# Another memory layout for the low magnitude rows and the short exponential tables of an S4 mixer kernel, and a written-down instruction sequence

## The chip, the cores and the metric

One NeuronCore of one Trainium2 chip runs the whole kernel. Its engines have instruction queues of their own and run side by side: TensorE (PE, whose weight loads are the row PEld), VectorE (DVE), ScalarE (ACT), GpSimd (POOL, nearly unused here) and SyncE (SP, which issues transfers). Each engine takes its queue strictly in order. The metric is the device time of one execution in microseconds.

## The reference

The input `x` has 2048 positions of 512 channels. It is normalised, and two branches work on the result.

- Branch A is a state-space convolution. Each channel `d` has 128 complex modes `n`, and its kernel is `K[d, l] = Re sum_n C[d,n] dB[d,n] exp(dt[d] A[d,n] l)` for `l = 0..2047`. The normalised input is convolved with `K` (in the reference with FFTs of length 4096), and `Dskip * u` is added.
- Branch B is a mixer with an MLP: layer norm, a 512x512 product, GELU, a shift of four channel groups by +1, -1, +2, -2 positions, a second 512x512 product and a residual; then layer norm, a product to 1376 features, GELU, a product back to 512 and a residual.

The output is `x + A * silu(B)`.

## The kernel before

**Stages.** The kernel first normalises, runs branch B's token mixing (`token_mixing`) and the first stage of the transform of the input (`u_stage1`, `u_spectra`). `tables(0)` and `tables(1)` build the kernel `K` for the two halves of the channels, each in eight chunks (`cc`) of 32 channels. `mlp(g)` is the MLP for one of eight groups of 256 positions; its products are two-part f16 products (`w3h`, `w4h`, `ghl`, `x1T`). `kstage1` and `products` transform `K` and multiply the spectra; `inverse` and `finish` come last.

**Tables.** The modes lie on the 128 partitions. A position is split in a coarse part, `256 a + 64 b` with a = 0..7 and b = 0..3, and a fine part of 64 values, so that the sum over modes becomes 64 small products per chunk (PE `pc<-pt`), of coarse factors with fine factors. Every factor is a magnitude (an exponential, from ACT) times a sine or cosine. The magnitudes are made once for a block of 128 channels, four blocks in all, by `block`:

- `mag` holds 64 rows of 128 channels, as two tiles of 32 rows: `mag[0]` (rows 0 to 31, the low rows) and `mag[1]` (rows 32 to 63). In each, row `4 b + c` of channel `q` stands at `[b, q, c]`: four rows lie side by side in memory, and the next channel is four words on. `exps` computes 40 of the 64 rows, each with one exponential of 128 channels, which writes every fourth word. `squares` makes the other 24 from these by squaring, in four instructions.
- `EB` holds 12 exponentials of 128 channels: `ea` (8 coarse steps a, with a innermost) and `eb` (4 steps b, with b innermost). `eb` is then multiplied by the mode's weight `wmr` (DVE `EB<-EB,par`).

Each chunk uses them on DVE: `factors` multiplies `ea` by `eb` (DVE `pt<-EB`, 1024 elements), and `sums` multiplies fine cosines and sines by `mag`. The four products of a chunk have 1024 elements each: `kf[:, low]` and `pf[:, low]` with `mag[0]`, `kf[:, mid]` with `mag[1]` (these three are DVE `TENSOR_TENSOR pt<-mag,pt`), and `pf[:, mid]` with `mag[1]` (DVE `SCALAR_TENSOR_TENSOR pt<-mag,pt`). Their outputs run over `[b, q, c]`, c innermost, because the matmuls read one channel at a time. The products' line in the profile is that of the helper that issues every instruction (L515), so tiles name the work.

**Order.** Nothing runs as the program records it. `Plan` records operations (some 1730) with their dependencies; `order` then gives each an engine and a place; `issue` writes each engine's queue in that order. Some operations can go to ACT or DVE (`Either`: copies, scalings by a constant, absolute values), some stores to SP or ACT. Before the change, `order` is a list scheduler: whenever an engine is free it takes, among the operations whose inputs are done by its own estimates, the one with the smallest due time in a table `DUE`, with extra costs for a change of ACT's table and preferences for DVE or ACT:

```
t, e = min(
    (max(free[e], min(o.ready for o in pool)), e) for e, pool in pools.items() if pool
)
...
if pick is None or (v, o.idx) < score:
    pick, score = o, (v, o.idx)
```

`order` also adds filler matmuls (`<-ident`, L514) where it expects PE to idle. Its cost for a DVE operation (`dve_cost`) knows nothing of memory layout; that of an ACT operation (`act_cost`) knows the step of the output.

Of the kernel before, what the change touches and what calls it, by code (L numbers as in the profile page):

```python
# [10 lines left out]
F32 = mybir.dt.float32  # L11
# [8 lines left out]
P = 128  # L20
# [16 lines left out]
BQ = 128  # L37
# [55 lines left out]
class Op:  # L93
    __slots__ = (
        "eng", "alts", "calls", "cost", "deps", "succ", "table", "vt", "idx", "nbytes", "n", "ready", "start",
        "alias", "first", "last", "psum", "mode", "stage", "dma", "room", "fresh", "free_at", "fill",
# [23 lines left out]
SHIFT, KEEP = 0.09, 1.0  # L120
# [6 lines left out]
DUE = (  # L127
# [129 lines left out]
)  # L257
SWITCH = 20.74
PREFERP, AVOIDP = 12.42, -13.86
PREFER, AVOID = -0.38, -5.84  # L260

# [1266 lines left out]
```

## Time and profile before

| | |
|---|---|
| median of 3 runs | 562.91 us (561.33 to 565.46) |
| the profiled execution's own time | 561.96 us |
| its span, first to last instruction | 560.2 us |
| PE busy / DVE busy / ACT busy | 533.4 / 466.1 / 410.2 us |
| granted TensorE clock, mean | 0.983 |
| ACT table loads | 49, 1283 ns each |

The profiled execution lies 0.95 us below the median of the runs; 1.76 us of its time lie outside the span. In the rows, a tile's buffer numbers are left out, `128x1024 f32` is partitions by elements, and "mean ns" is an instruction's own duration: on DVE and ACT the next instruction starts somewhat before the last one ends, so instructions in a row stand closer than their durations. Busy time in a stretch counts such overlap once.

### The profile page before, as it was taken

What the parts mean: (1) busy time and instruction counts of PE and PEld (TensorE: products, weight loads), DVE (VectorE), ACT (ScalarE), POOL (GpSimd) and SP (SyncE); (2) the same over time, 40 slices, a digit from 0 to 9 for tenths busy, and PEclk for the clock granted to TensorE, in tenths of its full rate; (3) what the DMA queues carried; (4) which work ended last, traced back from release to release, by engine and by line L of the source; (5) the groups of instructions that cost most, each with busy time, mean ns of one, the idle gap of its engine ahead of it and who ended that gap; (6) DMA issues with size and microseconds to landing.
All of it is one profiled execution on the core that took longest, in us unless ns stands there. A gap on an engine that the chain in (4) does not pass through costs nothing.

```text
span 560.2 us, 14282 instructions
## 1 busy us (share of the span) xinstructions
PE 533.4 (95%) x6104; PEld 349.6 (62%) x6104; DVE 466.1 (83%) x710; ACT 410.2 (73%) x588; POOL 0.7 (0%) x6
## 2 busy tenths in 40 slices
PE   7989999989899899999999999999999999999982
PEld 7967677855344466656766666676676665675630
DVE  5999999999999998999999999999415168564276
ACT  2999997999987998998899999768246235224420
POOL 0000000000000000000000000000000000000000
PEclk9999999999999899999999999999999999999995
DMA  9975667535647252735333431453886669859947
GB/s 205 229 214 190 233 222 253 180 117 165 196 143 263 96 140 68 217 140 186 112 100 100 133 131 60 142 162 124 264 281 236 225 190 281 254 156 277 327 130 223
DMA packets 69695, 103.14 MB, mean 184 GB/s; under 512 B 14784, under 2 KB 48832, under 8 KB 68736
## 3 DMA queue, kind: packets, MB, share of 16 engines
q1 hardware_dynamic: 68864, 100.13, 57.8%
q10 hardware_dynamic: 768, 2.10, 1.2%
q8 instruction: 48, 0.79, 0.6%
q14 instruction: 15, 0.12, 0.1%
HBM read 64.46 MB, written 37.75 MB: 182 GB/s over the span
## 4 chain that ended last, share of the span: by engine, by line
PE 72%; DVE 15%; ACT 5%; DMA 5%; issue 2%; SPq 1%; DVEq 0%; ACTq 0%
PE pb L515 29%; PE pa L515 21%; PE pd L515 11%; PE pc L515 11%; DVE pt L515 9%; DVE X L515 3%; DMA X<-in_A_u_dram 2%; ACT mag L515 2%; DMA w<-in_B_w_dram 2%; ACT pt L515 1%; DVE w4h L515 1%; SPq L515 1%; ACT L512 1%; DVE w3h L515 1%; DMA out_dram<-X 0%
## 5 line engine op out<-in xcount | busy, mean ns | idle before, releaser
L515 PE MATMUL pb<-x1T,w3h 128*128 128x256 f16 (+1 forms) x1056 | 123.4, 273 | 2.7 <-issue 1.2
L515 PE MATMUL pa<-w4h,ghl 128*128 128x512 f16 (+1 forms) x528 | 121.7, 379 | 0.0
L515 PEld LDWEIGHTS <-w3h 128*128 128x128 f16 (+1 forms) x1056 | 102.6, 100 | 28.5 <-issue 13.9
L515 PEld LDWEIGHTS <-ghl 128*128 128x128 f16 (+1 forms) x528 | 49.9, 98 | 59.7 <-issue 7.5
L515 DVE SCALAR_TENSOR_TENSOR ghl<-g,wsc,ghl 128x512 f16<-128x512 f32 (+1 forms) x48 | 33.6, 700 | 41.7 <-ACT ghl L515 41.6
L512 ACT ACT_TABLE_LOAD x49 | 62.9, 1283 | 7.4 <-DMA out_dram<-X 5.8
L515 PE MATMUL pd<-w,hT 128*128 128x512 f32 x116 | 56.8, 633 | 5.3 <-DVE X L515 4.3
L515 PE MATMUL pb<-xT,w 128*128 128x256 f32 x256 | 59.6, 384 | 1.9 <-ACT hT L515 1.4
L515 ACT ACTIVATE pt<-pt 128x2048 f32<-128x2048 f32 x29 | 55.2, 1906 | 7.6 <-DVE pt L515 7.6
L515 DVE TENSOR_TENSOR pt<-mag,pt 128x1024 f32<-128x1024 f32 x48 | 57.5, 1214 | 0.0
L515 ACT ACTIVATE g<-pb,wsc 128x512 f32<-128x512 f32 (+1 forms) x48 | 30.8, 649 | 35.6 <-PE pb L515 33.8
L515 PEld LDWEIGHTS pb<-xT,w 128*128 128x128 f32 x256 | 47.1, 190 | 13.4 <-ACT hT L515 3.6
L515 ACT ACTIVATE ghl<-g,wsc 128x512 f16<-128x512 f32 (+1 forms) x41 | 28.0, 688 | 30.0 <-PE pa L515 29.7
L515 PEld LDWEIGHTS pd<-w,hT 128*128 128x128 f32 x116 | 22.4, 201 | 33.9 <-issue 26.1
L515 ACT ACTIVATE mag<-par 128x128 f32<-128x128 f32 x160 | 41.0, 452 | 0.2
L515 DVE TENSOR_TENSOR pt<-pt 128x2048 f32<-128x2048 f32 x16 | 36.5, 2280 | 0.0
L515 DVE SCALAR_TENSOR_TENSOR pt<-pt 128x2048 f32<-128x2048 f32 x16 | 36.4, 2277 | 0.0
L515 PEld LDWEIGHTS pc<-pt 128*32 128x32 f32 x2048 | 29.5, 110 | 7.9 <-issue 5.8
L515 PE MATMUL pc<-pt 128*32 128x64 f32 x2048 | 32.5, 220 | 0.0
L515 ACT ACTIVATE pt<-pt,halfpi 128x2048 f32<-128x2048 f32 x16 | 32.0, 1998 | 0.1
L515 DVE TENSOR_TENSOR pr<-pd,uin 128x1024 f32<-128x1024 f32 x16 | 18.9, 1218 | 10.9 <-PE pd L515 10.8
L515 ACT ACTIVATE pt<-pt,magic 128x2048 f32<-128x2048 f32 x12 | 24.0, 1996 | 4.6 <-DVE pt L515 4.6
(149 smaller groups left out, 773.8 us busy)
## 6 DMA issues: line engine op xcount, KB each, us to landing
wst<-in_B_w_dram SPq DMA_DIRECT2D x20, 512.0 KB, 4.2
scr_Ud<-ue SPq DMA_DIRECT2D x16, 512.0 KB, 3.2
uin<-scr_Ud SPq DMA_DIRECT2D x32, 256.0 KB, 4.3
cst<-c_gp SPq DMA_DIRECT2D x16, 384.0 KB, 3.7
scr_Uh<-uh SPq DMA_DIRECT2D x8, 512.0 KB, 3.6
scr_Kfa<-k1e SPq DMA_DIRECT2D x8, 512.0 KB, 2.6
kin<-scr_Kfa SPq DMA_DIRECT2D x16, 256.0 KB, 3.2
scr_Zda<-z1e SPq DMA_DIRECT2D x8, 512.0 KB, 4.7
```

Source lines behind the costliest of these rows:

```text
L512: self.engines["ACT"].preload_act_table_set(SETS[table])
L515: ins = [getattr(self.engines[op.eng], name)(*args, **kw).ins for name, args, kw in op.calls]
```

## The change

Three things change.

1. **Low rows.** `mag[0]` lies in memory as `[b, c, q]`: each of its 32 rows is 128 words in one piece. The view that the products read is still `[b, q, c]`, so two elements that follow each other are now 128 words (512 bytes) apart in memory. `mag[1]` stays as it was. The squares that fill low rows write runs; those that fill `mag[1]` from low rows read with steps of 128 words.
2. **Short tables.** `ea` and `eb` lie as `[a, q]` and `[b, q]`. Their exponentials write runs; `EB<-EB,par` reads and writes with steps of 128 words, and `pt<-EB` reads `eb` with steps of 128 words, and `ea` with such a step after every fourth element (each value is used four times in a row).
3. **Order.** The scheduler's choice is gone. `SEQUENCE` lists all operations in the order in which they are issued, `CHOICE` gives the engine of each that could go to two. The estimates stay, since filler matmuls still come from them.

```
--- before.py
+++ after.py
-DUE = (
-    85.23, 583.2, 38.92, 85.35, 55.21, -217, -232.4, -232.7, -216.45, 35.93, 42.19, 33.18, -58.99, -322.42,
...
+SEQUENCE = (
+    16, 13, 50, 4, 39, 88, 2, 15, 0, 48, 14, 47, 3, 49, 12, 5, 19, 7, 6, 8, 17, 23, 22, 18, 24, 21, 27, 20, 44,
...
+CHOICE = (
+    "AAAAAAAADDAAAADADAADAADAADADAAADAADADDDADDADDADDAADDDDDDADDADAAAAADAAAAAADADAAAAAAAAADAAAAADAAADAADA"
...
+            if len(op.alts) > 1:
+                letter = next(choice)
+                op.eng = next(e for e in op.alts if e[0] == letter)
...
-        while len(out) < len(ops):
-            t, e = min(
-                (max(free[e], min(o.ready for o in pool)), e) for e, pool in pools.items() if pool
-            )
...
+        for k in SEQUENCE:
+            pick = ops[k]
+            assert pick.n == 0
+            e = pick.eng
+            t = max(free[e], pick.ready)
...
-        mag = [at(magn + 4 * K4 * h, [P, 8, BQ, 4], F32, "mag") for h in range(2)]
-        ea = EB[:, : 8 * BQ].rearrange("p (q a) -> p q a", a=8)
-        eb = EB[:, 8 * BQ :].rearrange("p (q b) -> p q b", b=4)
+        rows_of = at(magn, [P, 8, 4, BQ], F32, "mag")
+        mag = [rows_of.rearrange("p b c q -> p b q c"), at(magn + 4 * K4, [P, 8, BQ, 4], F32, "mag")]
+        ea = EB[:, : 8 * BQ].rearrange("p (a q) -> p q a", a=8)
+        eb = EB[:, 8 * BQ :].rearrange("p (b q) -> p q b", b=4)
...
-                A.activation(
-                    mag[b // 4][:, 2 * b % 8 + h : 2 * b % 8 + 2 * n : 2, :, 0:4:2],
-                    mag[0][:, b : b + n, :, 2 * h : 2 * h + 2], AF.Square,
-                )
+                src = rows_of[:, b : b + n, 2 * h : 2 * h + 2]
+                if b == 4:
+                    dst, src = mag[1][:, h : 2 * n : 2, :, 0:4:2], src.rearrange("p b c q -> p b q c")
+                else:
+                    dst = rows_of[:, 2 * b + h : 2 * b + 2 * n : 2, 0:4:2]
+                A.activation(dst, src, AF.Square)
```

Of the operations that can go to two engines, the new sequence puts on ACT what was on DVE: three copies `par<-pa`, one `ue<-pa`, one `z1e<-pd`, two `k1e` and one `kev`; and on DVE what was on ACT: nine scalings `ghl<-g` of 128x512 and one cast `x1T<-pb`.

The first place is ACT, at the third block of the tables: `EB` and `mag` are the exponentials and squares of `block`, `w3h` weights of the MLP, `x1n` and `x1T` the MLP's input, `kev` a chunk's finished part of `K`. Before:

```order
L515 ACTIVATE EB<-par 128x128 x12
L515 COPY kev<-pc 128x512
L515 ACTIVATE w3h<-wst,wsc 128x4x256
L515 ACTIVATE x1n<-X,bs,rs 128x512 x2
L515 ACTIVATE mag<-par 128x128 x16
L515 COPY kev<-pc 128x512
L515 ACTIVATE mag<-par 128x128 x8
L515 CAST x1T<-pb_97 128x4x128
L515 ACTIVATE w3h<-wst,wsc 128x4x256
L515 ACTIVATE mag<-par 128x128 x16
L515 ACTIVATE mag<-mag 128x2x256 x2
L515 ACTIVATE mag<-mag 128x4x256
```

The same place on ACT now:

```order
L455 ACTIVATE EB<-par 128x128 x12
L455 ACTIVATE w3h<-wst,wsc 128x4x256
L455 ACTIVATE x1n<-X,bs,rs 128x512
L455 COPY kev<-pc 128x512
L455 ACTIVATE x1n<-X,bs,rs 128x512
L455 ACTIVATE mag<-par 128x128 x16
L455 COPY kev<-pc 128x512
L455 ACTIVATE mag<-par 128x128 x8
L455 CAST x1T<-pb_97 128x4x128
L455 ACTIVATE w3h<-wst,wsc 128x4x256
L455 ACTIVATE mag<-par 128x128 x8
L455 ACTIVATE mag<-mag 128x2x2x128 x2
```

The exponentials, 52 of them in a block, stand in nearly the same places; a copy of `kev` moves back by two instructions, and the two short squares stand eight exponentials earlier. They write `2x2x128` (runs of 128) where they wrote `2x256`.

The second place is DVE, at the last chunk of the tables: `pr` are spectral products, `ghl` and `x1T` parts of the MLP, `rs` a small normalisation. Before:

```order
L515 SCALAR_TENSOR_TENSOR X<-pa,wsc,X 128x1024
L515 TENSOR_TENSOR pt<-mag,pt 128x1024
L515 TENSOR_TENSOR pt<-pt 128x2x1024
L515 SCALAR_TENSOR_TENSOR ghl<-g_396,wsc,ghl 128x512
L515 TENSOR_TENSOR pt<-mag,pt 128x1024 x2
L515 SCALAR_TENSOR_TENSOR pt<-mag,pt 128x1024
L515 TENSOR_TENSOR x1T<-pb_97,x1T 128x4x128
```

The same place on DVE now:

```order
L455 TENSOR_TENSOR pt<-mag,pt 128x1024
L455 TENSOR_TENSOR pt<-pt 128x2x1024
L455 SCALAR_TENSOR_TENSOR ghl<-g_396,wsc,ghl 128x512
L455 TENSOR_TENSOR pt<-mag,pt 128x1024
L455 SCALAR_TENSOR_TENSOR pt<-mag,pt 128x1024
L455 TENSOR_TENSOR pt<-mag,pt 128x1024
L455 TENSOR_TENSOR x1T<-pb_97,x1T 128x4x128
L455 SCALAR_TENSOR_TENSOR rs<-rs 128x2
L455 TENSOR_SCALAR ghl<-g_398,wsc 128x512
```

One of the chunk's products changes its place with its neighbour. The scaling `ghl<-g_398`, which was ACT's, is the first of the nine that move to DVE; all nine stand behind the last table product.

More of the change, by code (lines that the diff above doesn't have):

```diff
@@ L94 @@
     __slots__ = (
-        "eng", "alts", "calls", "cost", "deps", "succ", "table", "vt", "idx", "nbytes", "n", "ready", "start",
-        "alias", "first", "last", "psum", "mode", "stage", "dma", "room", "fresh", "free_at", "fill",
+        "eng", "alts", "calls", "cost", "deps", "succ", "table", "idx", "nbytes", "n", "ready", "start",
+        "alias", "first", "last", "mode", "dma", "room", "fresh", "free_at", "fill",
     )
@@ L119 @@
 ISSUE = 0.45
-SHIFT, KEEP = 0.09, 1.0
+SHIFT = 0.09
 FETCH = 1.3, 5.0, 2.5
@@ L125 @@
 UP, DOWN = 1.31, 1.297
-DUE = (
[129 rows of a table removed]
-)
-SWITCH = 20.74
-PREFERP, AVOIDP = 12.42, -13.86
-PREFER, AVOID = -0.38, -5.84
+SEQUENCE = (
[88 rows of a table added]
+)
+CHOICE = (
+    "AAAAAAAADDAAAADADAADAADAADADAAADAADADDDADDADDADDAADDDDDDADDADAAAAADAAAAAADADAAAAAAAAADAAAAADAAADAADA"
+    "AAADAAAAADAAAAAAADAAAAAAAAAAAAAAAADAADAAAAADAAADAAAAAAAAAAAAAAAAAAADAAADDAAAAAADDAAAAAAAADDAADADADDA"
+    "AADDAADDAADADADAAADADAAADAAAAADADDDDADADAADAAAADAAADSAAAASSASSASSAAAAAASAAASSASSAASS"
+)
 class Clock:
@@ L356, in new @@
         op = Op()
-        op.alts, op.table, op.dma, op.psum = {}, table, dma, False
+        op.alts, op.table, op.dma = {}, table, dma
         op.deps, op.alias, op.idx = set(), set(), len(self.ops)
-        op.vt = DUE[op.idx]
         op.room, op.fresh, op.mode = set(), True, 0
@@ L366, in add @@
         op = self.group or self.new(table, dma)
-        op.psum = "PSUM" in str(reads[0].space) if reads else False
         if "PE" in alts:
@@ L433, in order @@
                 ops[d].succ.append(op)
-        pools = {e: [] for e in self.engines}
         free = dict.fromkeys(self.engines, 0.0)
-        def release(op):
-            for e in op.alts:
-                pools[e].append(op)
+        choice = iter(CHOICE)
         for op in ops:
-            if op.n == 0:
-                release(op)
-        table, mode, chan, landed, clock, words, out = 0, 0, 0.0, [], Clock(), Fetch(), []
-        while len(out) < len(ops):
-            t, e = min(
-                (max(free[e], min(o.ready for o in pool)), e) for e, pool in pools.items() if pool
-            )
-            pick, score = None, None
-            for o in pools[e]:
-                if o.ready <= t + 0.02:
-                    v = o.vt
-                    if e == "ACT" and o.table and o.table != table:
-                        v += SWITCH
-                    if e == "PE" and o.mode != mode:
-                        v += KEEP
-                    if len(o.alts) > 1:
-                        on = (PREFERP, AVOIDP) if o.psum else (PREFER, AVOID)
-                        v += on[e != "DVE"]
-                    if pick is None or (v, o.idx) < score:
-                        pick, score = o, (v, o.idx)
-            for k in pick.alts:
-                pools[k].remove(pick)
-            pick.eng = e
+            if len(op.alts) > 1:
+                letter = next(choice)
+                op.eng = next(e for e in op.alts if e[0] == letter)
+            else:
+                op.eng = next(iter(op.alts))
+        table, mode, chan, landed, clock, words, out = 0, 0, 0.0, [], Clock(), Fetch(), []
+        for k in SEQUENCE:
[3 more added lines that the diff above has]
+            t = max(free[e], pick.ready)
             pick.cost, pick.calls = pick.alts[e]
@@ L500, in order @@
                     s.free_at = max(s.free_at, after)
-                if s.n == 0:
-                    release(s)
         self.span = max(max(free.values()), chan)
@@ L960, in squares @@
             for h in range(2):
-                A.activation(
-                    mag[b // 4][:, 2 * b % 8 + h : 2 * b % 8 + 2 * n : 2, :, 0:4:2],
-                    mag[0][:, b : b + n, :, 2 * h : 2 * h + 2], AF.Square,
-                )
+                src = rows_of[:, b : b + n, 2 * h : 2 * h + 2]
+                if b == 4:
+                    dst, src = mag[1][:, h : 2 * n : 2, :, 0:4:2], src.rearrange("p b c q -> p b q c")
+                else:
+                    dst = rows_of[:, 2 * b + h : 2 * b + 2 * n : 2, 0:4:2]
+                A.activation(dst, src, AF.Square)
         with plan.together(table=TABLES[AF.Exp]):
```

215 rows, old and new, of tables (DUE, SEQUENCE) are left out of this document.

## The prediction

> **What bounds the kernel now.** I read the page first. Its spans, its busy times by slice and the summary of the chain of waits:
>
> ```profile
> span 560.2 us, 14282 instructions
> PE 533.4 (95%) x6104; PEld 349.6 (62%) x6104; DVE 466.1 (83%) x710; ACT 410.2 (73%) x588; POOL 0.7 (0%) x6
> PE   7989999989899899999999999999999999999982
> DVE  5999999999999998999999999999415168564276
> ACT  2999997999987998998899999768246235224420
> PE 72%; DVE 15%; ACT 5%; DMA 5%; issue 2%; SPq 1%; DVEq 0%; ACTq 0%
> ```
>
> By shares this is a TensorE kernel. But each digit is a slice of 14 us, and DVE stands at nine (once at eight) from the second slice to the 28th: up to 392 us there are two full engines, after that one. So I asked for busy times by stretch (PE, PEld, DVE, ACT, POOL, each with its count):
>
> ```profile
> 28.00:112.00 84.00, 82.29 (x671) 61.84 (x672) 82.10 (x171) 78.91 (x108) 0.00 (x0) 1.00 0.68 215
> 112.00:196.00 84.00, 77.24 (x1010) 40.08 (x1009) 83.83 (x99) 78.02 (x119) 0.00 (x0) 0.96 0.50 164
> 196.00:224.00 28.00, 26.84 (x281) 17.38 (x280) 25.79 (x59) 26.41 (x62) 0.00 (x0) 1.00 0.40 104
> 224.00:392.00 168.00, 167.65 (x2318) 110.59 (x2317) 167.77 (x211) 153.03 (x185) 0.00 (x0) 1.00 0.41 134
> 392.00:532.00 140.00, 138.81 (x1402) 89.61 (x1401) 66.18 (x91) 53.92 (x68) 0.00 (x0) 1.00 0.79 249
> ```
>
> From 28 to 392 us DVE works 82.10 + 83.83 + 25.79 + 167.77 = 359.5 of 364 us: 4.5 us are free. PE idles 1.71 + 6.76 + 1.16 + 0.35 = 10.0 us there. After 392 us PE is busy for 138.81 of 140 us and DVE for 66.18; what DVE does not finish before 392 us finds room there, but PE, which takes its queue in order, would have to wait for it first. The chain of waits in order of time (start, length) says who is late in the middle:
>
> ```profile
> 152.96 7.67 DVE pt L515 x6
> 204.28 4.88 ACT mag L515 x18
> ```
>
> At 153 us it runs through DVE's table products, at 204 us through ACT's exponentials: the two sorts of work that the change touches.
>
> **Part 1: what the new layout costs DVE.** The tiles `mag` and `EB`, each group with its shortest, median and longest duration (ns), and the first and last start:
>
> ```profile
> L515 ACT ACTIVATE mag<-par x160: 414/452/485, 14.0 to 328.8; 128x128 f32<-128x128 f32 x160
> L515 DVE TENSOR_TENSOR pt<-mag,pt x48: 1201/1215/1226, 71.5 to 389.6; 128x1024 f32<-128x1024 f32 x48
> L515 DVE SCALAR_TENSOR_TENSOR pt<-mag,pt x16: 1203/1214/1219, 80.2 to 390.7; 128x1024 f32<-128x1024 f32 x16
> ...
> L515 ACT ACTIVATE EB<-par x48: 436/457/482, 17.8 to 294.1; 128x128 f32<-128x128 f32 x48
> L515 DVE TENSOR_TENSOR pt<-EB x16: 1202/1214/1218, 53.3 to 376.7; 128x1024 f32<-128x1024 f32 x16
> L515 DVE TENSOR_TENSOR EB<-EB,par x4: 673/681/683, 49.4 to 314.8; 128x512 f32<-128x512 f32 x4
> ```
>
> Of the 48 products `pt<-mag,pt`, two in three read low rows: 2 x 16 chunks = 32. With the 16 `pt<-EB`, 48 products of 1024 elements will read a word from a new place, 512 bytes on, at every element. Before, every operand in SBUF is read in runs of four words, or holds one word for four elements. All of them lie inside DVE's full stretch.
>
> No DVE instruction of before reads SBUF like that, so the price has to be bounded by neighbours. The groups by form, then the timeline (start, length):
>
> ```profile
> L515 DVE COPY kev<-pc 128x512 f32<-128x512 f32 x3 | 2.0, 680 | 0.0
> L515 DVE CAST x1T<-pb 128x512 f16<-128x512 f32 x3 | 2.0, 680 | 0.0
> L515 ACT ACTIVATE X<-X 128x1024 f32<-128x1024 f32 x8 | 8.5, 1059 | 0.8 <-DVE X L515 0.7
> L515 ACT ACTIVATE pt<-pt 128x2048 f32<-128x2048 f32 x29 | 55.2, 1906 | 7.6 <-DVE pt L515 7.6
> L515 ACT ACTIVATE mag<-mag 128x1024 f32<-128x1024 f32 x8 | 9.2, 1156 | 0.0
> L515 ACT ACTIVATE mag<-mag 128x512 f32<-128x512 f32 x8 | 5.1, 680 | 0.0
> L515 DVE COPY par<-pa 128x256 f32<-128x256 f32 x3 | 1.2, 408 | 0.0
> L515 DVE COPY ue<-pa 128x1024 f32<-128x1024 f32 x4 | 4.9, 1216 | 0.0
> ```
>
> ```profile
> 204.18 3.96 ACT L515 ACTIVATE mag<-par 128x128 f32<-128x128 f32 x16
> 211.67 0.69 ACT L515 ACTIVATE g<-pb,wsc 128x512 f32<-128x512 f32 x1
> 212.26 0.60 ACT L515 ACTIVATE w3h<-wst,wsc 128x384 f16<-128x384 f32 x1
> ...
> 369.30 2.35 DVE L515 TENSOR_TENSOR pt<-mag,pt 128x1024 f32<-128x1024 f32 x2
> ```
>
> - From below: the copy `kev<-pc` reads PSUM with a step of 64 words at every element, and takes 680 ns, as long as the cast that reads PSUM in runs. A hop costs DVE nothing there; but that is another memory. A gain is excluded: today's products already take one element after the other without a gap.
> - From above: ACT's exponentials of before write SBUF four or eight words apart. Sixteen take 3.96 us, so they follow each other by (3.96 - 0.452) / 15 = 0.234 us, which is 1.83 ns for each of 128 elements. How long would a run take? From 1024 to 2048 elements in runs ACT's duration grows by (1906 - 1059) / 1024 = 0.827 ns per element; 128 elements would last 1059 - 896 x 0.827 = 318 ns instead of 452, and start some 0.10 us before the last ends (211.67 + 0.69 against 212.26), so follow each other by about 0.218 us. Read by the spacing, a hop costs 0.016 us / 128 = 0.12 ns; read by the duration, 134 ns / 128 = 1.05 ns, which with 0.827 is again 1.87 ns per element.
>
> I take the rate of 1.83 ns per element: with 128 elements the slow words can hide under what an instruction costs anyway, with 1024 they can't, and this is the row of the same memory. DVE's two products in a row take 2.35 us, so follow each other by 2.35 - 1.215 = 1.135 us; at 1.83 ns it would be 1024 x 1.83 = 1.87 us, 0.74 us more. 48 x 0.74 = **35.5 us**. The four `EB<-EB,par` of 512 elements go from about 0.60 to 0.94 us: 4 x 0.34 = **1.3 us**. Together 36.8 us of DVE time, and the ends 0 and 36.8 stay for the range.
>
> The Trainium skill has a measured rule for just this ("Vector Engine (DVE) Microarchitecture Reference", section 5.2, Measured stream behaviour on trn2): a port keeps its full rate only while its elements come in adjacent pairs of words, and a two-source program with one source that hops at every element took 1.73 ns per column instead of 1.054. By that page the 48 products would cost 48 x 1024 x 0.676 ns = 33 us, an estimate that would put the kernel some 2 us lower than my sum; the products before, in runs of four words, agree with its full rate (1.135 us / 1024 = 1.11 ns), and no run so far shows its slow one.
>
> **Part 2: what the layout gives ACT.** In each of four blocks 24 of the 40 exponentials of `mag` and all 12 of `EB` become runs: 144 in all, 144 x 0.016 = 2.3 us. The eight short squares lose their step of two words (680 to about 640 ns): 0.3 us. The eight long squares, which now read with a step of 128 words, cost something between nothing and 1024 x (1.83 - 1.13) = 0.72 us each, 5.7 us. So ACT's sum lies between -2.6 and +3.1 us. ACT is idle for 6 of 84 us and 15 of 168 us in the two long stretches, which covers either; only from 196 to 224 us is it late, by one block, a quarter of that. I take nothing.
>
> **Part 3: the new order.** Counted up to the last table product, these leave DVE: three `par<-pa` (0.41 us), one `ue<-pa` (1.22), one `z1e<-pd` of the same size, two `kev<-pc` (0.68) and one cast `x1T<-pb` (0.68): 1.2 + 1.2 + 1.2 + 1.4 + 0.7 = **5.7 us** less. A `kev` and two casts come back behind that product, where the two `k1e` leave. The nine scalings `ghl<-g` that come to DVE stand behind the last table product, where DVE is idle half the time. PE has as much to do as before. Nor does the order change the stages: the last chunk's products stand behind the same MLP pieces. What the shuffled neighbours bring I bound by PE's 10.0 us of idle time, with a loss of the same sort of 3 us; I take nothing.
>
> **What becomes of DVE's delay.** Part of it is swallowed by lead, that is by the time between a chunk's last product and its matmuls:
>
> ```profile
> 355.66 1.22 DVE L515 SCALAR_TENSOR_TENSOR pt<-mag,pt 128x1024 f32<-128x1024 f32 x1
> 374.91 1.22 DVE L515 TENSOR_TENSOR pt<-mag,pt 128x1024 f32<-128x1024 f32 x1
> 390.73 1.21 DVE L515 SCALAR_TENSOR_TENSOR pt<-mag,pt 128x1024 f32<-128x1024 f32 x1
> ...
> 363.57 1.99 PE L515 MATMUL pc<-pt 128*32 128x64 f32 x128
> 378.81 1.99 PE L515 MATMUL pc<-pt 128*32 128x64 f32 x128
> 393.47 1.99 PE L515 MATMUL pc<-pt 128*32 128x64 f32 x128
> ```
>
> The leads are 6.7, 2.7 and 1.5 us, 3.6 us in the mean. Everything queued behind a slow product on DVE waits with it: `ghl` and `x1T`, on which PE's MLP products wait, and the spectral products `pr`. So PE stands still for what is left: 36.8 - 5.7 (moved off) - 4.5 (DVE's free time) - 3.6 (lead) = **23.0 us**. After the tables PE's 139 us of work follow unchanged. Against the profiled execution, 561.96 us, that is 585.0; against the median, which lies 0.95 us higher, **586 us**.
>
> **Rivals.**
>
> - *DVE slows down as computed* (the forecast). For it: the ACT rows, and that DVE has 4.5 us free. With half the price (18.4 us) and the longest lead, 18.4 - 5.7 - 4.5 - 6.7 = 1.5: 564 us. With nothing swallowed, ACT late by a quarter of its 3.1 us, and the order's 3 us: 36.8 + 0.8 + 3 - 5.7 = 34.9, 598 us. Its own range is 564 to 598. Chance 0.68.
> - *Faster: the hop costs DVE nothing*, as it costs nothing with PSUM. Then DVE has 5.7 us less and ACT 2.6 us less in stretches where PE waits for them, and PE can win back at most its 10.0 us of idle time. I take 5.7 + 2.6 = 8.3, less the 3 us that a changed order may lose: 5.3, 557.6 us, between 553 and 563. It decides if the price of a hop lies below about 0.1 ns per element. The same page of the Trainium skill speaks a little for it: a one-source stream that changed between two places at every element ran at the full rate. Chance 0.22.
> - *No change: the hop costs what ACT's spacing shows*, 0.12 ns per element, 48 x 1024 x 0.12 = 6 us on DVE, which the 5.7 us moved off and the 4.5 us of free time cover: 560 to 566 us. Chance 0.10.
>
> That the layout might not reach the instructions is excluded: the product of `EB` is `128x128x4` in the new queue and was `128x512`.
>
> **How the numbers follow.** One per cent of 562.9 us, about what a measurement of this kernel can tell from no change, is 5.6 us: 557.3 to 568.5. Faster: half of the second case, since its time lies at that bound, and a little for an order better than I see, 0.13. Same: the rest of the second (0.09), the third (0.10) and the lowest 0.02 of the first, 0.21. Slower: 0.66. The likeliest time is 586 us. For 8 in 10 the range reaches from 556, which leaves out the better third of the second case (0.08), to 598 (leaving out 0.05 and with it some 0.05 of what I don't see).
>
> **What would show it.** If I am right, the groups by form show two prices for `pt<-mag,pt`: 16 products near 1.2 us and 32 near 1.9 us, `pt<-EB` near 1.9 us, and DVE's busy time is some 33 us higher, with PE idle by some 23 us more before the last `pc<-pt`, which would start near 416 us. The forecast falls if these products stay at 1.2 us, or if they take 1.9 us and the last `pc<-pt` still starts near 395 us. ACT's exponentials in runs should last near 0.32 us, and the long squares tell what a hopping read costs ACT.

## The result and the profile after

The changed kernel takes **595.15 us** (median of 4 runs, 594.16 to 598.37), the kernel before 562.12 us beside it (560.05 to 565.46): a ratio of 1.059, 95% interval 1.055 to 1.063. The forecast was 586 us, with a range of 556 to 598: the sign is right, the time is 9 us too low. The profiled execution of the changed kernel is the slowest of its four, 598.37 us; from profile to profile the span grows by 36.4 us, by the medians the time grows by 33.0.

The page of the changed kernel, with its span, busy times, slices and chain of waits (the helper that issues every instruction is now L455, and L454 or L458 in some kernels below):

```profile
span 596.6 us, 14264 instructions
PE 542.2 (91%) x6106; PEld 352.1 (59%) x6106; DVE 507.1 (85%) x712; ACT 404.7 (68%) x586; POOL 0.7 (0%) x6
PE   7999999789799698998989999999899999999982
DVE  5999999999999999899999999999944238654476
DVE 56%; PE 28%; DMA 6%; issue 5%; ACT 3%; SPq 1%; DVEq 0%; ACTq 0%
```

PE held 72% of the chain before and DVE 15%; now it is 28% and 56%. DVE's row of nines now ends with the 29th slice of 14.9 us; it ended with the 28th of 14.0 us. DVE's busy time grew by 41.0 us and ACT's fell by 5.5.

The groups by form (busy us, mean ns of one), first of the kernel before, then of the changed one:

```profile
L515 DVE TENSOR_TENSOR pt<-mag,pt 128x1024 f32<-128x1024 f32 x48 | 57.5, 1214 | 0.0
L515 DVE TENSOR_TENSOR pt<-EB 128x1024 f32<-128x1024 f32 x16 | 19.3, 1213 | 0.0
L515 ACT ACTIVATE mag<-par 128x128 f32<-128x128 f32 x160 | 41.0, 452 | 0.2
```

```profile
L455 DVE TENSOR_TENSOR pt<-mag,pt 128x1024 f32<-128x1024 f32 x48 | 81.8, 1725 | 0.6 <-ACT pt L455 0.5
L455 DVE TENSOR_TENSOR pt<-EB 128x1024 f32<-128x1024 f32 x16 | 33.6, 2106 | 0.0
L455 DVE TENSOR_TENSOR EB<-EB,par 128x512 f32<-128x512 f32 x4 | 4.3, 1064 | 0.0
L455 ACT ACTIVATE mag<-par 128x128 f32<-128x128 f32 x160 | 36.8, 356 | 7.7 <-DVE pt L455 7.6
L455 ACT ACTIVATE mag<-mag 128x1024 f32<-128x1024 f32 x8 | 10.3, 1283 | 0.0
L455 ACT ACTIVATE EB<-par 128x128 f32<-128x128 f32 x48 | 10.0, 294 | 0.0
```

The products with `mag` cost 24.3 us more, those of `EB` 14.3, and the four `EB<-EB,par`, 681 ns each before, 1.5 to 1.6 more: **40.1 us** by busy times. The mean of 1725 ns mixes two prices. The groups of the tile `mag` show them (shortest, median, longest):

```profile
L455 DVE TENSOR_TENSOR pt<-mag,pt x48: 1201/1952/2076, 78.6 to 427.2; 128x1024 f32<-128x1024 f32 x48
L455 DVE SCALAR_TENSOR_TENSOR pt<-mag,pt x16: 1202/1222/1271, 82.4 to 426.1; 128x1024 f32<-128x1024 f32 x16
```

`mag[1]` kept its layout, and its products stay at 1.2 us. The timeline of the changed kernel (start, length, and what a wait ended on) gives the rates by spacing, and the end of the tables:

```profile
15.59 2.49 ACT L455 ACTIVATE EB<-par 128x128 f32<-128x128 f32 x12
339.82 4.10 DVE L455 TENSOR_TENSOR pt<-EB 128x1024 f32<-128x1024 f32 x2
402.01 3.84 DVE L455 TENSOR_TENSOR pt<-mag,pt 128x1024 f32<-128x1024 f32 x2
427.21 1.22 DVE L455 TENSOR_TENSOR pt<-mag,pt 128x1024 f32<-128x1024 f32 x1
428.49 1.99 PE L455 MATMUL pc<-pt 128*32 128x64 f32 x128 [1.78 <-DVE pt L455]
```

Two low products follow each other by 3.84 - 1.95 = 1.88 us, that is 1.84 ns per element (1.11 before); two `pt<-EB` by 4.10 - 2.11 = 1.99 us, 1.95 ns. By spacing the change costs DVE 32 x (1.88 - 1.135) + 16 x (1.99 - 1.135) + 4 x 0.38 = 39.0 us. ACT's exponentials in runs follow each other by (2.49 - 0.294) / 11 = 0.200 us.

The last `pc<-pt` starts at 428.49 us instead of 393.47, **35.0 us later**, directly at the end of the last product: the lead of 1.5 us is gone. What follows it lasts 168.1 us instead of 166.7. So nearly the whole loss lies ahead of this matmul. Busy times by stretch (PE, PEld, DVE, ACT, POOL, then granted clock):

```profile
28.00:428.00 400.00, 365.15 (x4316) 233.82 (x4315) 396.31 (x532) 340.40 (x482) 0.00 (x0) 0.97 0.45 143
428.00:568.00 140.00, 138.39 (x1385) 89.26 (x1386) 70.22 (x101) 46.38 (x58) 0.00 (x0) 1.00 0.78 241
```

The same of the kernel before, up to the end of its tables:

```profile
28.00:392.00 364.00, 354.01 (x4275) 229.88 (x4276) 359.49 (x537) 336.37 (x472) 0.00 (x0) 0.99 0.49 157
```

DVE is idle for 3.7 of 400 us, PE for 34.9; before it was 4.5 and 10.0 of 364. ACT, with less to do, waited more. Two of its waits for DVE in the changed kernel (total, times, longest), and the first of them before:

```profile
ACT pt L455 <- DVE pt L455: 26.2, 15, 4.7
ACT mag L455 <- DVE pt L455: 7.6, 4, 4.6
```

```profile
ACT pt L515 <- DVE pt L515: 12.2, 9, 3.8
```

The first was 12.2 us; the second is new, and ends when DVE has read the `mag` that the next exponentials overwrite.

### The profile page after: what moved, and what is told of

It is laid out like the page before. It is cut to its first block, busy times and chain, and to the rows that moved or that the text cites. A ratio compares the mean times of both kernels' runs of the same rounds, so it can differ in the third digit from the quotient of the medians.

```text
span 596.6 us, 14264 instructions
## 1 busy us (share of the span) xinstructions
PE 542.2 (91%) x6106; PEld 352.1 (59%) x6106; DVE 507.1 (85%) x712; ACT 404.7 (68%) x586; POOL 0.7 (0%) x6
## 4 chain that ended last, share of the span: by engine, by line
DVE 56%; PE 28%; DMA 6%; issue 5%; ACT 3%; SPq 1%; DVEq 0%; ACTq 0%
DVE pt L455 32%; PE pa L455 10%; PE pb L455 10%; PE pc L455 5%; DVE X L455 5%; DVE pr L455 5%; PE pd L455 3%; DVE stats L455 2%; DVE ghl L455 2%; DMA X<-in_A_u_dram 2%; DMA wst<-in_B_w_dram 2%; DMA uin<-scr_Uh 1%; DVE rs L455 1%; DVE pab L455 1%; ACT pt L455 1%
## 5 line engine op out<-in xcount | busy, mean ns | idle before, releaser
L455 PE MATMUL pa<-w4h,ghl 128*128 128x512 f16 (+1 forms) x528 | 124.5, 380 | 2.1 <-DVE ghl L455 2.0
L455 PE MATMUL pb<-x1T,w3h 128*128 128x256 f16 (+1 forms) x1056 | 124.0, 273 | 0.6 <-DVE x1T L455 0.6
L455 PEld LDWEIGHTS <-w3h 128*128 128x128 f16 (+1 forms) x1056 | 103.1, 100 | 25.5 <-issue 9.0
L455 PEld LDWEIGHTS <-ghl 128*128 128x128 f16 (+1 forms) x528 | 49.2, 98 | 63.8 <-issue 11.1
L455 DVE TENSOR_TENSOR pt<-mag,pt 128x1024 f32<-128x1024 f32 x48 | 81.8, 1725 | 0.6 <-ACT pt L455 0.5
L452 ACT ACT_TABLE_LOAD x49 | 62.9, 1283 | 9.2 <-DVE X L455 7.7
L455 PE MATMUL pd<-w,hT 128*128 128x512 f32 x116 | 57.9, 643 | 9.9 <-DVE X L455 9.8
L455 ACT ACTIVATE pt<-pt 128x2048 f32<-128x2048 f32 x29 | 55.3, 1906 | 10.9 <-DVE pt L455 10.9
L455 ACT ACTIVATE g<-pb,wsc 128x512 f32<-128x512 f32 (+1 forms) x48 | 30.6, 648 | 46.7 <-PE pb L455 45.2
L455 PE MATMUL pb<-xT,w 128*128 128x256 f32 x256 | 61.3, 389 | 0.4 <-ACT xT L455 0.4
L455 PEld LDWEIGHTS pb<-xT,w 128*128 128x128 f32 x256 | 47.7, 193 | 13.4 <-issue 4.3
L455 PEld LDWEIGHTS pd<-w,hT 128*128 128x128 f32 x116 | 22.9, 206 | 39.0 <-issue 25.9
L455 DVE SCALAR_TENSOR_TENSOR ghl<-g,wsc,ghl 128x512 f16<-128x512 f32 (+1 forms) x48 | 33.5, 700 | 14.4 <-ACT ghl L455 14.0
L455 ACT ACTIVATE mag<-par 128x128 f32<-128x128 f32 x160 | 36.8, 356 | 7.7 <-DVE pt L455 7.6
L455 PE MATMUL pc<-pt 128*32 128x64 f32 x2048 | 34.4, 222 | 6.3 <-DVE pt L455 6.0
L455 PEld LDWEIGHTS pc<-pt 128*32 128x32 f32 x2048 | 30.3, 111 | 15.2 <-DVE pt L455 8.2
L455 DVE SCALAR_TENSOR_TENSOR pt<-pt 128x2048 f32<-128x2048 f32 x16 | 36.6, 2286 | 0.0
L455 DVE TENSOR_TENSOR pt<-pt 128x2048 f32<-128x2048 f32 x16 | 36.6, 2291 | 0.0
L455 ACT ACTIVATE ghl<-g,wsc 128x512 f16<-128x512 f32 (+1 forms) x32 | 21.7, 677 | 20.5 <-PE pa L455 19.4
L455 DVE TENSOR_TENSOR pr<-pd,uin 128x1024 f32<-128x1024 f32 x16 | 19.0, 1220 | 18.7 <-PE pd L455 13.6
L455 ACT ACTIVATE pt<-pt,magic 128x2048 f32<-128x2048 f32 x12 | 24.0, 2003 | 15.0 <-DVE pt L455 15.0
L455 DVE TENSOR_TENSOR pt<-EB 128x1024 f32<-128x1024 f32 x16 | 33.6, 2106 | 0.0
```

Source lines behind the costliest of these rows:

```text
L452: self.engines["ACT"].preload_act_table_set(SETS[table])
L455: ins = [getattr(self.engines[op.eng], name)(*args, **kw).ins for name, args, kw in op.calls]
```

## The experiments

Theory: DVE is the engine that paces the tables, the hopping read costs it 0.74 us for 1024 elements, and what this adds appears in the time, less a little slack. Rivals: the new order, or ACT, sets the time; or it is not the hop that costs.

### The layout apart from the order

**Written order, layout of before** (`block` has its four old view lines and old squares):

```
-        rows_of = at(magn, [P, 8, 4, BQ], F32, "mag")
-        mag = [rows_of.rearrange("p b c q -> p b q c"), at(magn + 4 * K4, [P, 8, BQ, 4], F32, "mag")]
+        mag = [at(magn + 4 * K4 * h, [P, 8, BQ, 4], F32, "mag") for h in range(2)]
-        ea = EB[:, : 8 * BQ].rearrange("p (a q) -> p q a", a=8)
-        eb = EB[:, 8 * BQ :].rearrange("p (b q) -> p q b", b=4)
+        ea = EB[:, : 8 * BQ].rearrange("p (q a) -> p q a", a=8)
+        eb = EB[:, 8 * BQ :].rearrange("p (q b) -> p q b", b=4)
```

> The written-down order of the change, with all tables in the layout of before. If the layout is the whole loss (the theory), the 48 products and the four products of EB fall back to 1.2 and 0.68 us, DVE's busy time falls by 24.3 + 14.3 + 1.5 = 40 us to about 467 us, and the kernel lands between 555 and 563 us. If the new order costs a part of its own (rival), it stays above 568 us.

562.98 us, ratio 1.000 (0.9985 to 1.002). The tiles' groups, the last table product and matmul, and the busy times up to 392 us of this kernel:

```profile
L455 DVE TENSOR_TENSOR pt<-mag,pt x48: 1195/1220/1226, 76.4 to 391.3; 128x1024 f32<-128x1024 f32 x48
L455 DVE TENSOR_TENSOR pt<-EB x16: 1201/1219/1225, 57.7 to 378.0; 128x1024 f32<-128x1024 f32 x16
391.30 1.22 DVE L455 TENSOR_TENSOR pt<-mag,pt 128x1024 f32<-128x1024 f32 x1
393.46 1.99 PE L455 MATMUL pc<-pt 128*32 128x64 f32 x128
28.00:392.00 364.00, 350.58 (x4278) 229.33 (x4278) 357.70 (x531) 339.79 (x481) 0.00 (x0) 1.00 0.49 156
```

The last `pc<-pt` stands where it stood before, to 0.01 us.

**New layout, order of before** (the old scheduler's sequence and choices, written down):

```
-    16, 13, 50, 4, 39, 88, 2, 15, 0, 48, 14, 47, 3, 49, 12, 5, 19, 7, 6, 8, 17, 23, 22, 18, 24, 21, 27, 20, 44,
...
+    88, 2, 13, 4, 0, 3, 39, 16, 1, 14, 15, 7, 6, 5, 8, 19, 17, 50, 20, 47, 21, 48, 22, 49, 18, 51, 23, 26, 52,
...
-    "AAAAAAAADDAAAADADAADAADAADADAAADAADAADDDADDADDADDAADDDDDDADDADAAAAADAAAAAADADAAAAAAAAADAAAAADAAADAADA"
...
+    "AAADDDAADDAAAADADAADAADADDAAAADAADAADADDADDADDADDAADDDDDDADDDDADAAADAAAAAADADAAAAAAAAADAAAAADAAADAADA"
...
```

> The order of before, instruction for instruction, with the new layout. Theory (the layout is the loss, in any order): 590 to 602 us, since the old order leaves 5.7 us more work on DVE before the last table product. Rival (the new order fits the slow products badly, and another order would hide them): under 585 us.

595.81 us, ratio 1.057 (1.054 to 1.060). Busy times up to the end of its tables, and the last table matmul:

```profile
28.00:428.00 400.00, 364.60 (x4318) 234.56 (x4318) 397.77 (x535) 334.85 (x473) 0.00 (x0) 0.97 0.44 142
427.81 0.32 PE L454 MATMUL pc<-pt 128*32 128x64 f32 x8
428.34 1.88 PE L454 MATMUL pc<-pt 128*32 128x64 f32 x120 [0.21 <-DVE pt L454]
```

So the layout is the whole loss, and the order is worth nothing in either layout. The 5.7 us of copies that the new order takes from DVE show as 397.77 - 396.31 = 1.5 us of DVE's busy time, and DVE is idle for as much more; of the last chunk's 128 matmuls 8 go ahead at 427.81 us here, and the other 120 start at 428.34 us, against 428.49 for all of them in the changed kernel. With the old layout it is the same: 359.49 - 357.70 = 1.8 us less busy, and 6.3 instead of 4.5 us idle. Part of the rest is seen in the sums of the rows by group. With the new layout DVE's instructions up to 428 us sum to 446.2 us here and to 436.6 in the changed kernel, 9.6 less, but neighbours overlap less there, so that the stretch they occupy shrinks by 1.5 us only. With the old layout the sums up to 392 us are 398.1 and 395.4 us, 2.7 less, since most of the remaining instructions last some nanoseconds longer in the written order (`stats<-X` 689 instead of 675). Why they overlap less or last longer is open.

### How much of DVE's time appears in the end

**Low rows alone in the new layout** (`ea` and `eb` as before), and **`eb` alone in the new layout** (everything else as before). Both have the written order; their edits are given against the first kernel above, and the squares of the first go with its layout:

```
-        mag = [at(magn + 4 * K4 * h, [P, 8, BQ, 4], F32, "mag") for h in range(2)]
+        rows_of = at(magn, [P, 8, 4, BQ], F32, "mag")
+        mag = [rows_of.rearrange("p b c q -> p b q c"), at(magn + 4 * K4, [P, 8, BQ, 4], F32, "mag")]
```

> The change without the new layout of EB: only the low rows are runs. DVE loses 14.3 us of the products pt<-EB and 1.5 us of EB<-EB,par. Theory (DVE's extra time passes to the span one to one): 596 - 16 = 580 us, between 577 and 583. Rival (part of the delay is waiting that comes with any late DVE): more than 586 us; other rival (the first 20 us of delay are hidden): under 572 us.

```
-        eb = EB[:, 8 * BQ :].rearrange("p (q b) -> p q b", b=4)
+        eb = EB[:, 8 * BQ :].rearrange("p (b q) -> p q b", b=4)
```

> The old layout but for eb, whose four steps lie as runs [b, q]: pt<-EB then hops 512 bytes at every element in eb alone, ea stays in runs of eight. What is open is why pt<-EB took 2.11 us in the changed kernel while the low products took 1.95. Theory 'the two hopping operands add up a little': with eb alone it takes 1.96 us like the low products, EB<-EB,par 1.06 us. Rival 'the additional time is eb's own' (its element is used by eight steps of ea): 2.11 us again. Time: 16 x 0.74 + 4 x 0.38 = 13.4 us more on DVE; by the 0.8 that low rows alone passed on, 563 + 10.7 = 573 to 576; the rival 576 to 577.

Low rows alone: 581.7 us, ratio 1.033 (1.029 to 1.037). `eb` alone: 571.77 us, ratio 1.015 (1.010 to 1.020), below what either theory gave. Their last table matmuls, in this order, and with `eb` alone the group of `pt<-EB`:

```profile
413.13 1.99 PE L455 MATMUL pc<-pt 128*32 128x64 f32 x128 [1.76 <-DVE pt L455]
```

```profile
404.02 1.99 PE L455 MATMUL pc<-pt 128*32 128x64 f32 x128 [0.54 <-DVE pt L455]
L455 DVE TENSOR_TENSOR pt<-EB x16: 1899/1967/2025, 57.5 to 388.8; 128x1024 f32<-128x1024 f32 x16
```

The busy times of the kernels with no hopping operand, with `eb` and with the low rows, and a table of all four:

```profile
PE 531.2 (95%) x6106; PEld 350.1 (63%) x6106; DVE 468.9 (84%) x712; ACT 406.3 (73%) x586; POOL 0.7 (0%) x6
PE 538.9 (94%) x6106; PEld 352.6 (62%) x6106; DVE 481.6 (84%) x712; ACT 407.2 (71%) x586; POOL 0.7 (0%) x6
PE 539.2 (93%) x6106; PEld 352.1 (61%) x6106; DVE 491.7 (85%) x712; ACT 404.3 (70%) x586; POOL 0.7 (0%) x6
```

| hopping operands | DVE busy, us | more than without | last `pc<-pt`, us | later | difference |
|---|---|---|---|---|---|
| none | 468.9 | | 393.46 | | |
| `eb` | 481.6 | 12.7 | 404.02 | 10.6 | 2.1 |
| low rows | 491.7 | 22.8 | 413.13 | 19.7 | 3.1 |
| all (the change) | 507.1 | 38.2 | 428.49 | 35.0 | 3.2 |

What is swallowed is not a share, it is 2 to 3 us, whatever the amount: the lead of the last chunk, and a little free time. I had put it at four fifths for `eb` from the row of the low rows; the table says a fixed piece and then one for one. With `eb` alone `pt<-EB` takes 1.967 us, not 2.108: the rest belongs to `ea`, whose hop after every fourth element adds 0.14 us.

**`ea` alone in the new layout** (8 of the 52 exponentials of a block, 32 in all four blocks):

```
-        ea = EB[:, : 8 * BQ].rearrange("p (q a) -> p q a", a=8)
+        ea = EB[:, : 8 * BQ].rearrange("p (a q) -> p q a", a=8)
```

> The written-down order, mag and eb as before, only ea (32 of the 52 exponentials of a block's runs and steps) laid out as runs. pt<-EB then reads eb in runs of four, and ea with a step of 128 words after every fourth element. Theory (only a hop at every element costs): pt<-EB stays at 1.21 us, and the time is that of the old layout in this order or up to 2 us less. Rival (a hop after four elements costs too, a quarter of the price): pt<-EB near 1.4 us and 3 us more.

562.01 us, ratio 0.998 (0.996 to 1.000). The rows of tile and group:

```profile
L455 DVE TENSOR_TENSOR pt<-EB x16: 1202/1221/1230, 58.7 to 379.0; 128x1024 f32<-128x1024 f32 x16
L455 ACT ACTIVATE EB<-par 128x128 f32<-128x128 f32 x48 | 11.0, 345 | 0.0
```

By itself `ea`'s hop, at which each word serves four elements in a row, costs DVE nothing; it costs only where `eb` hops at every element as well. ACT gets 12.3 - 11.0 = 1.3 us back, and the interval just reaches 1.

### What it is in the hop that costs

Three kernels have `ea` in the new layout and `eb` in the old one, and change how the low rows lie or are read.

**Pairs**: two rows of a channel lie side by side, so that ACT writes every second word, and each low product is two instructions of 512 elements:

```
+        rows_of = at(magn, [P, 8, 2, BQ, 2], F32, "mag")
+        mag = [rows_of.rearrange("p b x q y -> p b q x y"), at(magn + 4 * K4, [P, 8, BQ, 4], F32, "mag")]
...
-        V.tensor_mul(kf[:, low], mag[0], kf[:, 15:7:-1, :, ::-1])
+        with plan.together():
+            for x in range(2):
+                V.tensor_mul(kf[:, low, :, 2 * x : 2 * x + 2], mag[0][:, :, :, x], kf[:, 15:7:-1, :, ::-1][:, :, :, 2 * x : 2 * x + 2])
```

> A middle layout: low rows in pairs, [b, pair, q, 2], so that the products read two adjacent words before each hop of 256 words, and the exponentials write every second word; ea in runs as in the run before, eb as before. Each low product is split in two instructions of 512 elements. Theory (a hop after every second element costs DVE nothing): the halves take 0.68 us and follow each other by 0.60, DVE has about 2 us more than with the old layout, and the kernel lands at 560 to 565 us, ACT's low exponentials standing some 0.21 us apart instead of 0.234. Rival (each hop costs the same, so pairs pay half): the halves near 0.85 us, 12 us more on DVE, 571 to 575 us.

564.29 us, ratio 1.002 (1.000 to 1.003). Four halves in a row, and ACT's exponentials:

```profile
369.86 2.50 DVE L455 TENSOR_TENSOR pt<-mag,pt 128x512 f32<-128x512 f32 x4
L455 ACT ACTIVATE mag<-par 128x128 f32<-128x128 f32 x160 | 36.8, 363 | 0.1
14.04 1.72 ACT L455 ACTIVATE mag<-par 128x128 f32<-128x128 f32 x8
```

A half lasts 0.69 us, as an instruction of 512 elements in runs does (`EB<-EB,par` before, 0.681 us): full speed. The halves follow each other by (2.50 - 0.69) / 3 = 0.60 us, so that two take 1.21 us where one whole product took 1.135, 0.07 us more; 32 x 0.07 = 2.2 us is about what DVE is busier than with the old layout (470.7 against 468.9 us). ACT's exponentials are as cheap as in the changed kernel (36.8 us in both, here (1.72 - 0.32) / 7 = 0.20 us apart where they write every second word), and nothing is gained: the 4.3 us that ACT loses of its busy time (406.3 to 402.0) lie off the path. The Trainium skill ("Vector Engine (DVE) Microarchitecture Reference", section 5.2, Measured stream behaviour on trn2) says that a port keeps its rate while elements come in adjacent pairs; this run agrees. For one source that hops at every element the page has 1.73 ns per column; the traces here show 1.84, and that decides for this kernel.

**Channel innermost in the product too**: `mag` is read in runs, the output and the sine or cosine every fourth word.

```
-        V.tensor_mul(kf[:, low], mag[0], kf[:, 15:7:-1, :, ::-1])
+        V.tensor_mul(*[t.rearrange("p b q c -> p b c q") for t in (kf[:, low], mag[0], kf[:, 15:7:-1, :, ::-1])])
```

> Low rows in runs as in the change (EB as before), but the low products run with the channel innermost: mag is read in runs, while the output is written and the sine or cosine read every fourth word (16 bytes). Theory (a hop costs on whichever operand makes it, short or long): the products stay at 1.9 us or above, 580 to 600 us. Rival (only the long hop costs): 1.2 us and about 562 us.

583.6 us, ratio 1.037 (1.034 to 1.039).

**A hop of 4096 bytes** instead of 512:

```
-        rows_of = at(magn, [P, 8, 4, BQ], F32, "mag")
+        rows_of = at(magn, [P, 4, 8, BQ], F32, "mag").rearrange("p c b q -> p b c q")
```

> Low rows in runs, but in the order [c, b, q], so that each hop of the low products is 4096 bytes instead of 512 (EB as before). Theory (the price is per hop, not per distance): products at 1.96 us, and the time of the run with low rows alone, 581.7 us, within 3 us. Rival (the price hangs on the distance): products 0.1 us or more away from 1.96 us, 4 us or more on the kernel.

581.79 us, ratio 1.033 (1.029 to 1.037). Low products two in a row and their group, of the former and of the latter:

```profile
388.36 4.04 DVE L455 TENSOR_TENSOR pt<-mag,pt 128x1024 f32<-128x1024 f32 x2
L455 DVE TENSOR_TENSOR pt<-mag,pt x48: 1203/2070/2183, 76.1 to 413.1; 128x1024 f32<-128x1024 f32 x48
```

```profile
388.92 3.84 DVE L455 TENSOR_TENSOR pt<-mag,pt 128x1024 f32<-128x1024 f32 x2
L455 DVE TENSOR_TENSOR pt<-mag,pt x48: 1205/1959/2075, 76.2 to 413.2; 128x1024 f32<-128x1024 f32 x48
```

With medians of 2.07 and 1.96 us, these are 1.97 and 1.88 us apart. Distance doesn't matter between 512 and 4096 bytes, and steps of 16 bytes on the output and the other source cost a little more. What costs is a step to a lone word at every element, and it can't be handed to the other two operands together; which of them costs more wasn't tried.

### Is DVE the only engine that paces?

**More DVE work behind the tables** (layout of before): the 16 spectral products of the second half of the channels are made twice, into the same place, which leaves the result as it is.

```
-            V.tensor_mul(t[0], kp, kh)
-            V.tensor_mul(t[1], kp, kh[:, :, ::-1])
+            for k, x in ((0, kh), (1, kh[:, :, ::-1])):
+                with plan.together():
+                    for _ in range(1 + hf):
+                        V.tensor_mul(t[k], kp, x)
```

> Old layout, written-down order, and DVE made to do the 16 spectral products of the second half twice: 16 x 1.14 = 18 us more DVE work, all behind the last table product. Theory (a DVE delay costs where DVE is full, before the tables end, and nearly nothing after): 563 to 569 us. Rival (any DVE work on the way to PE costs one to one): 578 us or more.

574.0 us, ratio 1.019 (1.018 to 1.021). A miss for both: 11 us come through of the 19.1 that DVE is busier than in the written order without the doubling. A stretch behind the tables, and PE's waits in this part (total, times, longest):

```profile
392.00:532.00 140.00, 130.89 (x1351) 84.51 (x1350) 85.67 (x111) 42.14 (x54) 0.00 (x0) 1.00 0.71 222
PE pd L455 <- DVE pr L455: 4.5, 5, 1.0
PE pc L455 <- DVE pr L455: 4.3, 4, 1.5
```

PE waits 8.8 us for these products in pieces of a microsecond, which it doesn't without the doubling, although DVE has room (85.67 of 140 us busy). Free time in a sum covers only work that nobody waits for soon.

**Angles on ACT**: seven shifts and absolute values of the angles (`pt<-pt`, 128x2048) go from DVE to ACT, once with the new layout and once with the old one.

```
                 op.eng = next(e for e in op.alts if e[0] == letter)
+                name = op.alts.get("DVE", (0, [("", ())]))[1][0]
+                if name[0] == "tensor_scalar" and columns(name[1][0]) == 2048:
+                    op.eng = "ACT"
```

> The changed kernel, with the seven shifts and absolute values of angles that DVE did (pt<-pt, 128x2048, 1.2 us each) on ACT instead: DVE has 8.4 us less before the last table product, ACT 13.4 us more. Theory 'DVE alone binds until the tables end': what leaves DVE is gained, 0.8 to 1 of 8.4 us, 586 to 589. Rival 'both engines are full together, so no other split pays': ACT gets late with tables and MLP, 594 or more.

> The same seven operations moved to ACT, with the layout of before and the written order. Theory 'DVE binds before the change too': 555 to 560. Rival 'before, PE, DVE and ACT are balanced up to 392 us (PE idles 10 us there), and time taken from DVE alone is worth nothing': 562 to 566.

New layout: 596.11 us, ratio 1.059 (1.055 to 1.063), no gain. Old layout: 577.16 us, ratio 1.024 (1.021 to 1.028), worse than either theory gave. A wait of DVE in the first and in the second, and the second's busy times up to the end of its tables:

```profile
DVE pt L458 <- ACT pt L458: 6.3, 5, 2.9
```

```profile
DVE pt L458 <- ACT pt L458: 15.1, 9, 4.6
28.00:407.00 379.00, 356.04 (x4306) 231.59 (x4305) 351.86 (x526) 351.92 (x488) 0.00 (x0) 0.99 0.47 150
```

DVE has 8.4 us less to do, and with the new layout waits 6.3 us for ACT (0.5 in the changed kernel), which works on the same chain of angles and takes its queue in order; with the old layout 27 of 379 us are idle. The last `pc<-pt` starts at 426.65 us with the new layout, 1.8 us earlier than in the changed kernel, and at 407.19 us with the old one, 13.7 us later than in the written order. So "DVE alone binds" is too simple: DVE and ACT hand a chunk to and fro, and time taken from DVE is not gained where DVE then waits for ACT. An order made for this split might do better; that wasn't tried. No kernel here beats the one before.

## Why the prediction was right, and where it was short

- **What binds.** Right: up to 392 us DVE had next to no free time, and what was added to its table work came out at the end. PE's idle time up to the last `pc<-pt` grew by 24.9 us, near the 23.0 that I worked out; but PE was also busy some 11 us longer with nearly the same matmuls, at a granted clock of 0.97 instead of 0.99, so this agreement doesn't confirm the sum. DVE's busy time grew by 41.0 us, not by some 33; 2.8 us of it came with the order (466.1 to 468.9 with the old layout). The start of the last `pc<-pt`, forecast at 416 us and found at 428.5, does show the miss.
- **The price of the low products.** Right: 1.84 ns per element against 1.83 taken, 0.745 us more against 0.74. That it equals the pace at which ACT writes every fourth word was a guess that held; the runs don't show that it is one mechanism, and ACT's own hopping reads are cheap (below).
- **The price of `EB`.** Too small: 0.855 us by spacing instead of 0.74, since I passed over `ea`'s additional hop. This is 1.8 us. The term of 36.8 us was 39.0 by spacing and 40.1 by busy time.
- **Moved off, -5.7 us.** Wrong, and the largest miss: the copies did leave DVE, but with either layout its busy time up to the end of the tables fell by 1.5 to 1.8 us only, its idle time rose by as much, and the last `pc<-pt` stayed within 0.2 us (with the new layout for 120 of its 128 matmuls).
- **Free time, -4.5 us.** Too much: in one and the same order the layout took 2.3 us of DVE's idle time (4.5 to 2.2, order of before) or 2.6 us (6.3 to 3.7, written order). Waits for inputs stay, such as the 0.6 us in the group of `pt<-mag,pt`.
- **Lead, -3.6 us.** Too much: I took the mean over three chunks, but the lead that counts is the last chunk's: 1.5 us in the kernel before, and 393.46 - 391.30 - 1.22 = 0.9 us in the written order with the old layout.
- **Together.** Order against like order, the terms nearly close: 39.0 - 2.6 - 0.9 = 35.5 us in the written order, against 35.0 found, and 39.0 - 2.3 - 1.5 = 35.2 us in the order of before, against 428.34 - 393.47 = 34.9. Of my 13.8 us of cover 3 to 4 were real, near the last column of the table. The forecast's 23.0 us were short by 12.0 in the profile, and by 10 of the 33.0 us by the medians.
- **ACT taken as nothing.** Right, although the saving was larger than the 2.3 us that I put: 144 exponentials at 0.200 instead of 0.234 us are 4.9 us. The long squares cost 8 x 0.13 = 1.0 us, near the lower end of my 0 to 5.7. `ea` alone and the pairs show no gain from such savings here.
- **The rivals.** "The hop costs nothing" fell for single words; it holds for pairs and for `ea`'s hop after every fourth element. "0.12 ns per element" fell for DVE. Both rested on rows of another memory or another engine.

## What to carry to other kernels

Look for the engine that pays for a layout, not only for the one that gains: here a run for the writer was a hop at every element for the reader, and the reader had 4.5 us to spare in 364. If a layout has to serve both sides, leave at least two neighbouring words on the side that reads; with pairs ACT wrote as cheaply as with runs and DVE read at full speed. When a delay hits a full engine, count as cover only the lead of the last consumer and idle time that isn't itself a wait; here 3 to 4 of 39 us.

## What the hardware showed that was not expected

- On ACT a read with a step of 128 words cost 1283 - 1156 = 127 ns for 1024 elements, 0.12 ns each, beside an output that steps by two words in both kernels; on DVE 0.73 ns each. What costs on ACT is writing words four or eight words apart: 452 to 457 ns for 128 elements, 294 ns in a run. Two words apart, as in the pairs, such instructions follow each other by 0.20 us, as in a run.
- On DVE an operand that hops after every fourth element costs nothing alone (1.221 us) and 0.14 us where the first hops at every element (2.108 against 1.967).
- In the long wait for DVE the granted clock of TensorE fell as well. From 196 to 224 us PE was busy for 22.30 of 28 us, at 0.88; before, it was 26.84 at full clock:

```profile
196.00:224.00 28.00, 22.30 (x310) 12.01 (x303) 28.00 (x41) 25.00 (x61) 0.00 (x0) 0.88 0.29 96
```

Since DVE was busy throughout that stretch, the slower clock is at most a part of the price; what it cost by itself wasn't measured.
